# Seven PSUM banks as one tensor, and two row maxima in one VectorE instruction

## The chip, the cores and the metric

The kernel runs on one core of a Trainium2 chip. A core has a matmul engine (PE, with its weight loads shown as PEld), a vector engine (DVE), a scalar engine (ACT), a general engine (POOL) and a queue engine for transfers (SP). Each works through its own instructions in order, and they meet through counters (semaphores): an instruction can wait until another engine's count has reached a value. Matmuls write into PSUM, which has eight banks of 512 f32 columns for each of 128 partitions. DVE and ACT read from there.

The metric is the device time of one execution in microseconds. The times of before are 2018.37, 2018.74 and 2018.93 us, median 2018.74.

## What is computed

One transformer block with adaptive layer norm. Six vectors come from `silu(c) @ w_mod`. Attention follows a modulated layer norm; then a mixing MLP with shifted channels follows another one.

```python
# S = 2048 tokens, D = 512, 32 heads of 16
h = layernorm(x) * (1 + ca) + sa
q, k, v = split_heads(h @ wqkv)                 # 32 x 2048 x 16 each
p = softmax(q @ k.T / 4)                        # 32 x 2048 x 2048
x = x + ga * (merge_heads(p @ v) @ wo)
h = layernorm(x) * (1 + cb) + sb
x = x + gb * mixer_and_mlp(h)                   # w1, shift, w2, w3, w4
```

The inputs make scores large, so the softmax subtracts the maximum of each row.

## The kernel before

There are three stages. A prologue norms and transposes x, makes the modulation and projects the first heads. The attention stage takes nearly three quarters of the time. The last stage, the tail, runs the output projection and the MLP.

Attention works on 64 units: four chunks of 512 queries times 16 pairs of heads. A unit has 16 steps `s`, one for each 128 keys, and in each step the two heads `j = 0, 1`. So there are 2048 half steps. For each of them two matmuls are made, on different halves of PE's rows:

- the maximum part (`max_part`, line 980): 128 queries times 512 keys into a bank called `mb` (line 996), from which DVE takes the maximum over the keys into one column of `mx` (line 992). It runs 24 steps (`LEAD`) ahead, since a unit's 32 maxima columns must be joined (`max_fin`, line 1029) and put into the query tile before its scores are made.
- the score part (`score_part`, line 998): 128 keys times 512 queries into a bank called `sc` (line 1012), of which ACT makes the exponential as int32 into a slot of `pt` (line 1008).

The int32 has a high half that is used as it is and a low half that must be turned to f16 first (`p_low`, line 1048): POOL does so for most steps (line 1061) and ACT for the others. Value matmuls then gather both halves in a bank `pv` of their own (lines 1083 and 1086); at the end of a unit ACT copies it out, four small matmuls `ot` add the parts, and ACT, DVE and POOL write the heads' output.

The program writes the order itself. A block is three half steps: three rows (`row_pair`, line 1014) of one maximum matmul and one score matmul, then the value matmuls of two blocks earlier. A class `Sched` keeps a modelled time for each engine. From these it decides when a block starts, whether a low half goes to POOL or ACT (`g > a + LACT`) and where other work, the fill, comes between blocks: projections of later heads, weight preparation, and at the end the first piece of the tail. `Slots` (line 305) keeps for each of the seven banks the modelled time from which it is free; any free bank will do, and each use makes a new tile with the tag of its bank:

```python
def bank(nm):
    x = sm.take()
    return x, ap_.tile([P, CH], F32, name=nm, tag=f"s{x}", bufs=1)
```

Fill work takes its banks from the same seven while attention runs (`dbank`, line 425). The eighth bank is `pv`.

The semaphore waits are not written in the kernel. The building layer derives them from which tile each instruction reads and writes.

Of the kernel before, what the change touches and what calls it, by code (L numbers as in the profile page):

```python
# [96 lines left out]
XCOPY = 0  # L97
NQ = 7
NPT = 6
NV = 3  # L100
DBW, DLAT = 360.0, 2200.0
NST = 4
# [9 lines left out]
class Sched:  # L112
# [29 lines left out]
    def chain(self, *ops, prio=1, ready=None, bank=None):  # L142

        if ready is None:
            ready = self.T["P"] + PX
        n = 0
        while n < len(self.chains) and self.chains[n][2] <= prio:
            n += 1
        bank = bank is not None and id(bank.tensor)
# [100 lines left out]
    def share(self, slots, most):  # L250

        self.avail, self.back, self.owner = [], [], {}
        self.slots, self.most = slots, most

    def take(self, tile):

        if self.slots:
            i = self.slots.take()
            self.slots.t[i] = LATE
        else:  # L260
            i = self.avail.pop(0)
        b = tile(i)
        self.owner[id(b.tensor)] = i
        self.open = id(b.tensor)
        return b

    def free(self, b):

        i = self.owner.pop(id(b.tensor), None)
# [35 lines left out]
class Slots:  # L305
# [7 lines left out]

    def late(self):
        return sum(t == LATE for t in self.t)


def cA(n=CH):
# [12 lines left out]
def kernel(ctx, tc, A_x, A_wqkv, A_wo, B_w1, B_w2, B_w3, B_w4, c, w_mod, out):  # L331
# [641 lines left out]
    sm = Slots(NSM)  # L973
    e_exp, e_hi, e_low, v_free, acs = {}, {}, {}, [0.0], []

    def bank(nm):
        x = sm.take()
        return x, ap_.tile([P, CH], F32, name=nm, tag=f"s{x}", bufs=1)

    def max_part(m, j):  # L980

        u, i = divmod(m, 16)
        c, g = divmod(i, 4)
        if u not in mxs:
            mxs[u] = at.tile([P, 2, 4, NC], F32, name="mx", tag="mx", bufs=2)
        x, b = bank("mb")
        ready, sm.t[x] = sm.t[x], LATE
# [3 lines left out]
        def after(e):  # L991
            end = sch.crit("D", 605, e + PX, lambda: dve.reduce_max(mxs[u][:, j, g, c:c + 1], b, axis=AX.X))  # L992
            sm.t[x] = end + XP["D"]
            if (c, g, j) == (NC - 1, 3, 0):
                max_fin(u)
        return ready, lambda: te.matmul(b, lhs, kst[u % 3][r, c * CH:(c + 1) * CH], start=True, stop=True), after  # L996

    def score_part(s, j):

        u, kt = divmod(s, NKT)  # L1000
        if j == 0:
            pt[s] = at.tile([P, 2, CH], I32, name="pt", tag="pt", bufs=NPT)
        x, b = bank("sc")
        ready, sm.t[x] = sm.t[x], LATE
        r = slice(64 * j, 64 * j + 64)

        def after(e):
            ea = sch.crit("A", 480, e + PX, lambda: act.activation(pt[s][:, j], b, AF.Exp))  # L1008
            sm.t[x] = ea + XP["A"]
            if j:  # L1010
                e_exp[s] = e_hi[s] = ea
        return ready, lambda: te.matmul(b, kst[u % 3][r, kt * P:(kt + 1) * P], qst[u][r], start=True, stop=True), after  # L1012

    def row_pair(s, j):

        parts = []
        if 0 <= s < NS:
            parts.append((j, score_part(s, j)))
        if s + LEAD < NS:
            parts.append((1 - j, max_part(s + LEAD, 1 - j)))  # L1020
        parts = [x for _, x in sorted(parts, key=lambda x: x[0])]

        def mms():
            for _, mm, _ in parts:
                mm()
        e = sch.put("P", CROW, max(x[0] for x in parts), mms)
        return [partial(x[2], e) for x in parts]

    def max_fin(u):
        mf = at.tile([P, 8], F32, name="mf", tag="mf", bufs=2)  # L1030
        nm = at.tile([P, 2, 8], F32R, name="nm", tag="nm", bufs=2)
        mx = mxs.pop(u)

        def shift_rows():
            for j in range(2):
                for i in range(2):
                    r = 64 * j + 62 + i
                    for h in range(2):
                        sch.dma(dma.dma_start,
                                qst[u][r:r + 1, h * 256:(h + 1) * 256].bitcast(F32).rearrange("o (p l) -> o p l", l=2),  # L1040
                                nm[:, i, 4 * j + 2 * h:4 * j + 2 * h + 2].bitcast(F32))
        sch.chain(("D", 85, lambda: dve.reduce_max(mf.rearrange("p (j g) -> p j g", j=2), mx, axis=AX.X)),
                  ("A", 100, lambda: act.activation(mf, mf, AF.Copy, scale=-1.0, bias=PEXP)),
                  ("A", 100, lambda: act.activation(nm[:, 0], mf, AF.Copy)),
                  ("G", 250, lambda: pool.tensor_tensor(nm[:, 1], mf, nm[:, 0], op=OP.subtract)),
                  (None, 0, shift_rows), mark(("shift", u)), prio=0, ready=sch.T["D"])

    def p_low(s):

        p = pt[s].rearrange("p j n -> p (j n)")  # L1050
# [17 lines left out]
    def pv_part(s, lo):  # L1068
# [7 lines left out]
        def mms():  # L1076
            for j in range(2):
                for i in range(2):
                    r = 64 * j + 32 * i
                    if lo:  # L1080
                        c = 128 + 32 * j + (0 if i else 8)
                        n = min(32, 192 - c)
                        te.matmul(acc[r:r + n, :], v[:, kt + i, c:c + n].bitcast(F16), pt[s + i].bitcast(F16)[:, j, 0::2],  # L1083
                                  start=False, stop=kt == NKT - 2, skip_group_check=True)
                    else:
                        te.matmul(acc[r:r + 32, :], v[:, kt, r:r + 32], pt[s].bitcast(F16)[:, j, 1::2],  # L1086
                                  start=kt == 0, stop=False, skip_group_check=True)
        e = sch.put("P", CCOL, 0.0, mms)
        if lo:
            for i in range(2):  # L1090
                pt.pop(s + i)
                e_low.pop(s + i)
            if kt == NKT - 2:
                acs.append((u, e + COUT))
# [507 lines left out]
    for k, blk in enumerate(blocks + [[]] * (LAG + CPER)):  # L1602
# [21 lines left out]
        banks = sorted(sm.t)  # L1624
        n = 0
        for s, i in row:
            n += (s >= 0) + (s + LEAD < NS)

            start = max(start, banks[n - 1 + 2 * (s < 0)] - t)
            t += CROW  # L1630
        t += CMID
        for s, i in col:
            start = max(start, pv_ready(s, i) - t)
# [2 lines left out]
        sch.flush(need)  # L1636
        sch.T["P"] = max(sch.T["P"], start) + CIN
        low = sorted(e_exp)
        for s, i in row:
            for fn in row_pair(s, i):  # L1640
                fn()
        for x in blk[1:]:
            if x % 2 == 0:
                before(x // 2)
# [86 lines left out]
```

## Time and profile before

| what | value |
|---|---|
| median of three runs | 2018.74 us |
| profiled execution, span | 2019.7 us |
| attention, first maximum to last small sum | 96.6 to 1536.5 us |
| PE busy | 1934.4 us, 96% |
| DVE busy | 1656.3 us, 82% |
| ACT busy | 1510.2 us, 75% |
| POOL busy | 1571.9 us, 78% |
| single maxima on DVE | 2048, 1250.0 us |
| exponentials on ACT | 2048, 1060.9 us |
| low halves on POOL and on ACT | 953, 1248.3 us, and 71 |

Busy times count an engine's records without overlap. The ends of matmuls are modelled, so 96% is not PE at its peak. A group's mean is the length of one record; busy time over count is what one costs in a stream where records overlap. Idle time stands with what ended it.

### The profile page before, as it was taken

How to read it: one execution, taken by the hardware profiler on the slowest of the kernel's cores; microseconds unless marked ns; L12 is line 12 of the kernel's file. 1: busy time of each engine (PE TensorE's matmuls, PEld its weight loads, DVE VectorE, ACT ScalarE, POOL GpSimd, SP SyncE). 2: the span in 40 equal slices, each digit the busy share in tenths (PEclk: the TensorE clock that was granted, in tenths of full speed). 3: DMA queues.
4: the chain of work that ended last, by engine and by line, in shares of the span. 5: the costliest groups of instructions: out<-in, count | busy, mean ns of one | idle time of the engine just before them, and what ended most of it. 6: DMA issues, size and time to landing. Idle time of an engine off the chain costs nothing.

```text
span 2019.7 us, 41655 instructions
## 1 busy us (share of the span) xinstructions
PE 1934.4 (96%) x14456; PEld 1162.1 (58%) x14456; DVE 1656.3 (82%) x2979; ACT 1510.2 (75%) x3085; POOL 1571.9 (78%) x1488
## 2 busy tenths in 40 slices
PE   7999999999999999999999999999998999999999
PEld 5755545454444444444444444444455878898998
DVE  6398888879999999999999999999975886556443
ACT  6438987768999999999999999999985544344443
POOL 6349988879999999999999999999996554435222
PEclk9989999999999999999999999999999999999999
DMA  8777675445343434444443435354414676553541
GB/s 295 233 204 192 151 187 155 135 130 124 86 92 87 91 88 83 96 82 97 81 98 75 104 72 107 72 136 126 99 46 158 230 261 265 226 200 116 201 153 68
DMA packets 185508, 278.01 MB, mean 138 GB/s; under 512 B 117104, under 2 KB 127856, under 8 KB 169008
## 3 DMA queue, kind: packets, MB, share of 16 engines
q1 hardware_dynamic: 181792, 267.20, 49.1%
q10 hardware_dynamic: 2304, 4.20, 0.6%
q0 software_dynamic: 1200, 3.93, 0.5%
q8 instruction: 115, 1.88, 0.4%
q14 instruction: 97, 0.79, 0.1%
HBM read 211.81 MB, written 62.91 MB: 136 GB/s over the span
## 4 chain that ended last, share of the span: by engine, by line
PE 61%; DVE 16%; ACT 9%; issue 6%; POOL 4%; DMA 3%; SPq 0%; ACTq 0%; POOLq 0%; DVEq 0%
PE mb L996 13%; DVE mx L992 12%; PE pv L1086 9%; PE sc L1012 8%; ACT pt L1008 7%; PE w L363 5%; PE w L359 5%; PE w L361 5%; PE pv L1083 4%; PE ot L1113 3%; POOL pt L1061 2%; PE xT L1247 1%; POOL trs L1356 1%; PE v L359 1%; DMA wr<-Ws 1%
## 5 line engine op out<-in xcount | busy, mean ns | idle before, releaser
L1061 POOL TENSOR_SCALAR pt<-pt 128x1024 f16<-128x1024 uint16 x953 | 1248.3, 1367 | 79.9 <-ACT pt L1008 76.7
L992 DVE TENSOR_REDUCE mx<-mb 128x1 f32<-128x512 f32 x2048 | 1250.0, 681 | 72.7 <-PE mb L996 63.5
L1008 ACT ACTIVATE pt<-sc 128x512 int32<-128x512 f32 x2048 | 1060.9, 614 | 123.5 <-PE mb L996 97.1
L996 PE MATMUL mb<-kst,qtl 62*128 62x512 f32 x2048 | 781.1, 461 | 20.5 <-ACT pt L1008 10.0
L1012 PE MATMUL sc<-qtl,kst 64*128 64x512 f32 x2048 | 739.3, 449 | 4.6 <-DVE mx L992 1.8
L996 PEld LDWEIGHTS mb<-kst,qtl 62*128 62x128 f32 x2048 | 358.9, 193 | 233.7 <-ACT pt L1008 160.4
L1012 PEld LDWEIGHTS sc<-qtl,kst 64*128 64x128 f32 x2048 | 336.6, 185 | 185.4 <-DVE mx L992 118.7
L1086 PE MATMUL pv<-pt,vst 128*32 128x512 f16 x4096 | 384.8, 397 | 20.6 <-ACT ac L1103 20.6
L1460 POOL TENSOR_TENSOR g<-sq,g 128x256 fp32r<-128x256 f32 (+1 forms) x124 | 96.8, 785 | 188.9 <-ACT g L1459 176.6
L1083 PE MATMUL pv<-pt,vst 128*32 128x512 f16 (+1 forms) x2048 | 220.8, 389 | 2.5 <-POOL pt L1061 2.4
L1086 PEld LDWEIGHTS <-vst 128*32 128x32 bf16 x4096 | 91.8, 93 | 227.2 <-issue 208.8
L361 PE MATMUL w<-A,wr 128*128 128x256 f32 (+1 forms) x520 | 153.4, 295 | 0.3 <-DVE A L349 0.3
L359 PE MATMUL w<-A,wr 128*128 128x256 f32 (+1 forms) x520 | 153.2, 295 | 0.3 <-ACT A L353 0.3
L363 PE MATMUL w<-A,wr 128*128 128x256 f32 (+1 forms) x520 | 153.1, 294 | 0.0
L1456 ACT ACTIVATE sq<-w 128x256 f32<-128x256 f32 (+1 forms) x130 | 52.1, 401 | 127.0 <-PE w L363 117.5
L363 PE MATMUL w<-wr,g 128*128 128x512 f32 x270 | 106.5, 394 | 3.1 <-POOL g L1460 3.1
L359 PE MATMUL w<-wr,g 128*128 128x512 f32 x270 | 106.9, 396 | 1.8 <-DMA wr<-Ws 1.8
L361 PE MATMUL w<-wr,g 128*128 128x512 f32 x270 | 106.1, 393 | 0.0
L1438 DVE SCALAR_TENSOR_TENSOR sq<-sq,w 128x256 f32<-128x256 f32 (+1 forms) x130 | 58.1, 449 | 56.5 <-ACT sq L1458 56.3
L359 PEld LDWEIGHTS w<-A,wr 128*128 128x128 f32 x520 | 98.7, 190 | 1.7 <-ACT A L353 0.5
L361 PEld LDWEIGHTS w<-A,wr 128*128 128x128 f32 x520 | 98.7, 190 | 1.6 <-DVE A L349 0.5
L363 PEld LDWEIGHTS w<-A,wr 128*128 128x128 f32 x520 | 98.6, 190 | 0.5 <-issue 0.5
(156 smaller groups left out, 2131.6 us busy)
## 6 DMA issues: line engine op xcount, KB each, us to landing
wr<-Ws SPq DMA_DIRECT2D x66, 1024.0 KB, 5.2
vst<-Vs SPq DMA_DIRECT2D x64, 768.0 KB, 5.7
kst<-Ks SPq DMA_DIRECT2D x126, 384.0 KB, 6.1
Ws<-wr SPq DMA_DIRECT2D x14, 1024.0 KB, 5.0
qtl<-Qs SPq DMA_DIRECT2D x128, 96.0 KB, 4.3
Vs<-vt SPq DMA_DIRECT2D x32, 384.0 KB, 4.2
Ks<-qk SPq DMA_DIRECT2D x16, 512.0 KB, 3.8
Qs<-qk SPq DMA_DIRECT2D x16, 512.0 KB, 3.0
```

Source lines behind the costliest of these rows:

```text
L359: te.matmul(o, lh, rh, start=first, stop=False)
L361: te.matmul(o, lh, rl, start=False, stop=False)
L363: te.matmul(o, ll, rh, start=False, stop=last)
L992: end = sch.crit("D", 605, e + PX, lambda: dve.reduce_max(mxs[u][:, j, g, c:c + 1], b, axis=AX.X))
L996: return ready, lambda: te.matmul(b, lhs, kst[u % 3][r, c * CH:(c + 1) * CH], start=True, stop=True), after
L1008: ea = sch.crit("A", 480, e + PX, lambda: act.activation(pt[s][:, j], b, AF.Exp))
L1012: return ready, lambda: te.matmul(b, kst[u % 3][r, kt * P:(kt + 1) * P], qst[u][r], start=True, stop=True), after
L1061: e_low[s] = XP["G"] + sch.crit("G", 1345, ready, lambda: pool.tensor_scalar(o, i, 0.5, 1.0, op0=OP.mult, op1=OP.mult))
L1083: te.matmul(acc[r:r + n, :], v[:, kt + i, c:c + n].bitcast(F16), pt[s + i].bitcast(F16)[:, j, 0::2], start=False, stop=kt == NKT - 2, skip ...
L1086: te.matmul(acc[r:r + 32, :], v[:, kt, r:r + 32], pt[s].bitcast(F16)[:, j, 1::2], start=kt == 0, stop=False, skip_group_check=True)
L1113: te.matmul(b[:, t * n:(t + 1) * n], ac[:, t * P:(t + 1) * P], smat.rearrange("p j d -> p (j d)"), start=True, stop=True)
L1460: ("G", cG(n), lambda: pool.tensor_tensor(lo, sq, hi, op=OP.subtract)), (None, 0, end), bank=b)
```

## The change

The seven banks become one PSUM tensor `psb` of seven slices of 512 columns. Maxima, scores and fill work all use slices of it. The six `pt` buffers become slots of one tensor `pts` in the same way.

In a block's three half steps the maxima are grouped: one goes alone, and two are put into adjacent slices and read by one reduction over `[128, 2, 512]` into two columns of `mx`. Its columns are put in a new order, so that the two lie side by side. `place` looks for slices that let the block start earliest, and `choose` falls back to three single maxima if pairing would start the block more than 150 ns later by the model (`DTOL`). Exponentials stay single (`DSC = 0`). The readers are put down after their last matmul; a pair of maxima comes after the second of its rows.

```diff
+DMX, DSC = 1, 0
+DTOL = 150.0
...
+    def key(self, b):
+        return id(b.tensor), b.offset
...
-        return sch.take(lambda i: psd["d"].tile([P, CH], F32, name=n, tag=f"s{i}" if psd["s"] else f"d{i}", bufs=1))
+        return sch.take(lambda i: psb[:, i] if psd["s"] else psd["d"].tile([P, CH], F32, name=n, tag=f"d{i}", bufs=1))
...
-    pv, pt = {}, {}
+    pv = {}
+    psb = ap_.tile([P, NSM, CH], F32, name="psb")
+    pts = at.tile([P, NPT, 2, CH], I32, name="pts")
...
+    def max_out(x, ts, e):
+
+        n = len(ts)
+        u, i = divmod(ts[0][0], 16)
+        o = 2 * i + 1 - ts[0][1]
+        b = psb[:, x:x + n]
+        end = sch.crit("D", 72 + 533 * n, e + PX, lambda: dve.reduce_max(mxs[u][:, o:o + n], b, axis=AX.X))
+        sm.t[x:x + n] = [end + XP["D"]] * n
+        if o + n == 32:
+            max_fin(u)
+
+    def score_out(x, ts, e):
+
+        n = len(ts)
+        s, j = ts[0]
+        o = 2 * (s % NPT) + j
+        p = pts.rearrange("p a j n -> p (a j) n")[:, o:o + n]
+        ea = sch.crit("A", 53 + 427 * n, e + PX, lambda: act.activation(p, psb[:, x:x + n], AF.Exp))
+        sm.t[x:x + n] = [ea + XP["A"]] * n
...
+    def groups_of(row, two):
+
+        ms = [(k, (s + LEAD, 1 - j)) for k, (s, j) in enumerate(row) if s + LEAD < NS]
+        ss = [(k, x) for k, x in enumerate(row) if x[0] >= 0]
+        out = []
+        for tiles, fn, fin, on, cut in ((ms, max_tile, max_out, DMX, lambda x: x[0] % NKT == 0 and x[1]),
+                                        (ss, score_tile, score_out, DSC, lambda x: x[0] % NPT == 0 and not x[1])):
+            i = 0
+            while i < len(tiles):
+                n = 2 if two and on and (len(tiles) - i) % 2 == 0 and not cut(tiles[i + 1][1]) else 1
+                out.append((tiles[i:i + n], fn, fin))
+                i += n
+        return sorted(out, key=lambda x: -len(x[0]))
+
+    def choose(row):
+
+        best = None
+        for two in (1, 0):
+            gs = groups_of(row, two)
+            st, xs = sm.place([[CIN + CROW * k for k, _ in ts] for ts, _, _ in gs], sch.T["P"])
+            if best is None or st + DTOL < best[0]:
+                best = st, gs, xs
+        return best
...
+        sch.chain(("D", 85, lambda: dve.reduce_max(mf.rearrange("p (j g) -> p j g", j=2),
+                                                   mx.rearrange("p (c g j) -> p j g c", g=4, j=2), axis=AX.X)),
...
+        if row:
+            row_pairs(row, *choose(row)[1:])
```

Counted in the built program, 2048 single maxima become 724 single ones and 662 pairs. The low halves that go to ACT fall from 71 to 17, and those on POOL rise from 953 to 1007. Matmuls and exponentials keep their number. `psb` is used by 8566 instructions; in the order in which they are put down its use passes from one engine to another 5625 times (2116 turns of PE, 2087 of ACT, 1423 of DVE).

Three places follow, as the program is built, with the counters that each instruction waits for. `PE_49`, `DVE_49`, `Activation_49` and `Pool_49` count the instructions of these engines, a `DMAHW` counter those of a transfer queue.

DVE in attention, before:

```order
L992 TENSOR_REDUCE mx<-mb 128x1 [waits DVE_49,PE_49]
L992 TENSOR_REDUCE mx<-mb 128x1 [waits PE_49]
L1042 TENSOR_REDUCE mf<-mx 128x8 [waits DVE_49,Pool_49]
L992 TENSOR_REDUCE mx<-mb 128x1 [waits PE_49] x30
L1128 RECIPROCAL rc<-sm 128x8 [waits Activation_49,Pool_49]
```

DVE in attention, now (`mx<-psb 128x2` is a pair):

```order
L1032 TENSOR_REDUCE mx<-psb 128x1 [waits PE_49,Activation_49]
L1032 TENSOR_REDUCE mx<-psb 128x2 [waits Activation_49]
L1032 TENSOR_REDUCE mx<-psb 128x1 [waits PE_49]
L1032 TENSOR_REDUCE mx<-psb 128x2 [waits PE_49,Activation_49]
L1108 TENSOR_REDUCE mf<-mx 128x8 [waits DVE_49]
L1032 TENSOR_REDUCE mx<-psb 128x1 [waits Activation_49]
L1032 TENSOR_REDUCE mx<-psb 128x2 [waits Activation_49]
```

Single maxima and pairs alternate, and a maximum now waits for ACT in many places where it waited for PE.

ACT in attention, before:

```order
L1008 ACTIVATE pt<-sc 128x512 [waits PE_49,Pool_49]
L1008 ACTIVATE pt<-sc 128x512 [waits PE_49] x3
L1008 ACTIVATE pt<-sc 128x512 [waits PE_49,Pool_49]
L1008 ACTIVATE pt<-sc 128x512 [waits PE_49]
L1008 ACTIVATE pt<-sc 128x512 [waits PE_49,Pool_49]
```

ACT in attention, now:

```order
L1043 ACTIVATE pts<-psb 128x512 [waits PE_49,Pool_49]
L158 ACTIVATE pts<-pts 128x1024 [waits Activation_49]
L1043 ACTIVATE pts<-psb 128x512 [waits DVE_49]
L1043 ACTIVATE pts<-psb 128x512 [waits PE_49,Pool_49]
L1043 ACTIVATE pts<-psb 128x512 [waits DVE_49]
L1043 ACTIVATE pts<-psb 128x512 [waits PE_49,Pool_49]
L1043 ACTIVATE pts<-psb 128x512 [waits DVE_49,PE_49]
```

An exponential now waits for DVE in many places where it waited for PE. (The `Pool_49` waits are for the slot that the exponential writes.)

PE, the three rows of a block, before and now (`kst` and `qtl` are the key and query tiles):

```order
L996 MATMUL mb<-kst_147,qtl_145 128x512 [waits Activation_49]
L1012 MATMUL sc<-qtl_1103,kst_1105 128x512 [waits DVE_49] x2
L996 MATMUL mb<-kst_147,qtl_145 128x512 [waits Activation_49] x2
L1012 MATMUL sc<-qtl_1103,kst_1105 128x512 [waits DVE_49]
L1086 LDWEIGHTS vst
```

```order
L1018 MATMUL psb<-kst_1063,qtl_1061 128x512 [waits DVE_49]
L1024 MATMUL psb<-qtl_965,kst_967 128x512
L1024 MATMUL psb<-qtl_965,kst_967 128x512 [waits Activation_49]
L1018 MATMUL psb<-kst_1063,qtl_1061 128x512
L1018 MATMUL psb<-kst_1063,qtl_1061 128x512 [waits Activation_49]
L1024 MATMUL psb<-qtl_965,kst_967 128x512
L1153 LDWEIGHTS vst
```

Before, each matmul waited for its own bank's reader; now the first matmul of each row waits and the second has no wait of its own.

More of the change, by code (lines that the diff above doesn't have):

```diff
@@ L148, in chain @@
             n += 1
-        bank = bank is not None and id(bank.tensor)
+        bank = bank is not None and self.key(bank)
         if bank == self.open:
@@ L315, in late, with place, go @@
         return sum(t == LATE for t in self.t)
+    def place(self, groups, now):
+        n = len(self.t)
+        best = [None, None]
+        def go(k, used, out, start, late):
+            if best[0] and start > best[0][0]:
+                return
+            if k == len(groups):
+                if best[0] is None or (start, late) < best[0]:
+                    best[:] = [(start, late), out]
+                return
+            offs = groups[k]
+            for i in range(n - len(offs) + 1):
+                if any(i + x in used for x in range(len(offs))):
+                    continue
+                st, lt = start, late
+                for x, o in enumerate(offs):
+                    st = max(st, self.t[i + x] - o)
+                    lt += self.t[i + x]
+                go(k + 1, used | {i + x for x in range(len(offs))}, out + [i], st, lt)
+        go(0, frozenset(), [], now, 0.0)
+        return (best[0][0] if best[0] else 2 * LATE), best[1]
 def cA(n=CH):
@@ L1090, in pv_part @@
             for i in range(2):
-                pt.pop(s + i)
                 e_low.pop(s + i)
@@ L1623 @@
         sch.flush(need)
[L1624 to L1630, printed above, removed]
+        if row:
+            start = choose(row)[0]
+            if s0 < 0:
+                start = max(start, sorted(sm.t)[need + 1] - t - CROW * (len(row) - 1))
+        t += CROW * len(row)
         t += CMID
```

80 lines of the change are left out of this document (35 added, 45 removed).

## The prediction

> **What bounds the kernel now.** I read the busy time by stretch first, to find the stage that the change touches. The columns are the stretch, its length, the busy time and instructions of PE, weight loads, DVE, ACT and POOL, the granted TensorE clock, and the DMA share and rate.
>
> ```profile
> 500.00:1450.00 950.00, 921.00 (x7837) 436.12 (x7830) 912.05 (x1587) 879.18 (x1743) 911.95 (x777) 1.00 0.44 94
> 96.60:1536.50 1439.90, 1393.33 (x11340) 690.01 (x11341) 1315.07 (x2281) 1245.82 (x2496) 1325.19 (x1137) 0.99 0.48 111
> 1536.50:2019.70 483.20, 457.58 (x2698) 409.36 (x2697) 294.16 (x589) 210.19 (x484) 201.00 (x286) 0.99 0.53 192
> ```
>
> Attention (first maximum to last small sum) is 1439.9 of the span's 2019.7 us, and in its steady part DVE, POOL, ACT and PE are all busy 93 to 97%: they run side by side. The groups of that part show what each does.
>
> ```profile
> L992 DVE TENSOR_REDUCE mx<-mb 128x1 f32<-128x512 f32 x1493 | 907.7, 681 | 31.6 <-PE mb L996 25.3 <-PE sc L1012 3.1
> L1061 POOL TENSOR_SCALAR pt<-pt 128x1024 f16<-128x1024 uint16 x684 | 890.4, 1363 | 32.8 <-ACT pt L1008 30.2
> L1008 ACT ACTIVATE pt<-sc 128x512 int32<-128x512 f32 x1493 | 770.0, 615 | 54.5 <-PE mb L996 44.9 <-PE sc L1012 2.2 <-POOL pt L1061 0.8
> L996 PE MATMUL mb<-kst,qtl 62*128 62x512 f32 x1493 | 574.8, 460 | 10.6 <-ACT pt L1008 6.9
> ```
>
> 1493 maxima are 497.7 blocks of three, so a block takes 950 / 497.7 = 1.91 us. A maximum costs DVE 907.7 / 1493 = 0.608 us of throughput, although a single one is recorded as 0.681: neighbours overlap at their ends. In the same way an exponential is 0.615 alone and 0.516 in the stream, and a POOL product 1.302. DVE fills 1.82 of the 1.91 us, POOL 1.85. The waits of the same stretch say how close the coupling is.
>
> ```profile
> PEld mb L996 <- ACT pt L1008: 137.4, 404, 0.8
> PEld sc L1012 <- DVE mx L992: 99.6, 258, 0.5
> ```
>
> PE waits for banks, 0.3 to 0.4 us at a time, so PE has slack. The kernel is bound by DVE and POOL, and it lives on ACT, DVE and PE working on different banks at the same time.
>
> **The change, part by part.**
>
> *The pair.* 662 pairs replace 1324 single maxima. A second 512 columns cannot cost more than a second instruction (0.608) or, in my reading of 0.681 alone against 0.608 streamed, much less than 0.53 (0.608 less the 0.073 by which two records overlap). So a pair saves DVE 0 to 0.075 us, at most 662 x 0.075 = 50 us of busy time.
>
> *POOL.* The order moves 54 of the 71 low-half products that ACT had taken back to POOL: 54 x 1.302 = 70 us more POOL work. If everything else stayed as it is, POOL would need 1.5 x 47/48 x 1.302 = 1.91 us a block plus what else it does (911.95 - 890.4 = 21.6 us in 497.7 blocks, 0.04), 1.95 in all against 1.91.
>
> *The one tensor.* This decides. In the rows of the order shown with the change, an exponential waits for DVE and a maximum for ACT; before, each of them waited for PE alone (and for the buffer it writes). I resolved every such wait to the instruction whose count it names. In all 5625 places where the use of `psb` passes from one engine to another, the first instruction of the new engine waits for the last one of the old, and about nine in ten of these waits join accesses to different banks. Readers wait for readers. So the seven banks are used by one engine at a time: row of matmuls, exponential, row, pair, exponential, row, and so on. What ran side by side is now a sum: 2116 turns of PE, and on ACT and DVE 2048 exponentials, 724 single maxima, 662 pairs and some 190 evictions of other work. That sum is what I price.
>
> *A turn of PE.* Here is a row of two matmuls at full clock, whose readers were waiting, and an exponential that released PE (time order: start, duration, engine, line, what).
>
> ```profile
> 534.16 0.18 PEld L1012 LDWEIGHTS sc<-qtl,kst 64*128 64x128 f32 x1 [0.45 <-DVE mx L992]
> 534.16 0.50 PE L1012 MATMUL sc<-qtl,kst 64*128 64x512 f32 x1
> ...
> 534.73 0.69 DVE L992 TENSOR_REDUCE mx<-mb 128x1 f32<-128x512 f32 x1 [0.42 <-PE mb L996]
> ...
> 534.76 0.60 ACT L1008 ACTIVATE pt<-sc 128x512 int32<-128x512 f32 x1 [0.42 <-PE mb L996]
> ```
>
> ```profile
> 1002.41 0.60 ACT L1008 ACTIVATE pt<-sc 128x512 int32<-128x512 f32 x1
> ...
> 1003.06 0.19 PEld L996 LDWEIGHTS mb<-kst,qtl 62*128 62x128 f32 x1 [0.30 <-ACT pt L1008]
> ```
>
> From PE's start to the waiting reader: 0.57 us to DVE, 0.60 to ACT, call it 0.585. An exponential alone takes 0.60 and PE starts 0.05 after its end: 0.65 a turn. I give DVE the same 0.05: 0.73 for a single maximum; and 0.681 + 0.53 + 0.05 = 1.26 for a pair (between 1.15, if it paid nothing but columns, and 1.41, twice a lone one).
>
> But the clock matters, because PE will mostly idle. Four neighbouring stretches of the clock's own length, and the row of matmuls in the slow one:
>
> ```profile
> 723.35:726.76 3.41, 3.41 (x34) 1.54 (x34) 3.41 (x7) 3.00 (x7) 3.41 (x4) 1.00 1.02 193
> 726.76:730.17 3.41, 2.25 (x22) 1.42 (x22) 2.23 (x4) 3.02 (x5) 2.50 (x3) 1.00 0.97 216
> 730.17:733.58 3.41, 3.41 (x17) 1.78 (x16) 2.52 (x5) 2.26 (x5) 2.99 (x4) 0.50 0.18 72
> 733.58:736.99 3.41, 3.41 (x34) 1.50 (x32) 3.38 (x8) 2.97 (x9) 2.74 (x3) 1.00 0.00 0
> ```
>
> ```profile
> 730.19 0.28 PEld L1012 LDWEIGHTS sc<-qtl,kst 64*128 64x128 f32 x1
> 730.19 0.79 PE L1012 MATMUL sc<-qtl,kst 64*128 64x512 f32 x1
> ...
> 731.05 1.89 DVE L992 TENSOR_REDUCE mx<-mb 128x1 f32<-128x512 f32 x3 [0.17 <-PE mb L996]
> 731.08 1.58 ACT L1008 ACTIVATE pt<-sc 128x512 int32<-128x512 f32 x3 [0.49 <-PE mb L996]
> ...
> 732.32 0.29 PEld L996 LDWEIGHTS mb<-kst,qtl 62*128 62x128 f32 x1 [0.44 <-ACT pt L1008]
> ...
> 733.15 1.29 DVE L992 TENSOR_REDUCE mx<-mb 128x1 f32<-128x512 f32 x2 [0.21 <-PE sc L1012]
> ```
>
> A stretch with 22 matmuls in place of 34 was followed by one at half clock; there a row takes 0.83 to 0.86 us to DVE and 0.89 to ACT, 0.865 as I use it. Half clock ended after a stretch of 17 slow but unbroken matmuls. In the changed kernel a block holds 6 row matmuls, 9 of the values and 0.4 small ones. With 6.6 us a block (below) that is 8 in 3.41 us, far under the 22 that lost the clock and the 17 that regained it. I take half clock through nearly all of attention.
>
> The Trainium skill ("TensorE: Matmul & The Clock Gate", section "Part 1: The HAM clock gate (the "warmup" mystery)") says that the gate falls to half rate after a whole idle window of about 3.4 us. Read so, PE, which works every two microseconds, would keep its full clock; the trace differs, since the stretch before 730.17 was busy for 2.25 of 3.41 us. What that reading would make of the time is the second rival.
>
> *Other work in the chain.* Projection and weight work of the first quarter takes its banks from `psb` too and stands in the chain: 312 matmuls of 512 columns, 252 of 256, 256 small ones. Two rows of the stream, and the small eviction:
>
> ```profile
> 97.83 0.28 PE L361 MATMUL v<-wp,hT 128*128 128x256 f32 x1
> ...
> 97.95 0.28 PE L363 MATMUL v<-wp,hT 128*128 128x256 f32 x1
> ```
>
> ```profile
> L1120 ACT ACTIVATE sm<-ot 128x136 f32<-128x136 f32 x47 | 13.4, 285 | 14.5 <-PE ot L1113 14.4
> ```
>
> 0.12 us for 256 columns, so 0.24 for 512, and double at half clock: 312 x 0.48 + 252 x 0.24 + 256 x 0.11 = 238 us. About 190 evictions at 0.29 to 0.6: 80 us.
>
> *The sum for attention:* PE turns 2116 x 0.865 = 1830; other matmuls 238; exponentials 2048 x 0.65 = 1331; single maxima 724 x 0.73 = 529; pairs 662 x 1.26 = 834; evictions 80. Together 4842 us. Over 699 blocks (683 of three scores each, and 16 at the start with maxima alone) that is 6.9 us with the extra work, 6.6 without (3 rows 2.6, 3 exponentials 1.95, a single and a pair 1.99). I take off 20 us for about 110 evictions that follow another on the same engine and overlap it by some 0.1 to 0.2. The value matmuls do not touch `psb`: per block nine, in groups of four side by side, about 1.1 us even at half clock (two and a quarter groups at twice the 0.23 between the two below). They lie behind the block's last row, under its exponential and maximum (0.65 + 1.26 = 1.9, or 0.65 + 0.73 = 1.4), so they cost nothing; without that cover they would be 1.1 us a block. POOL's 1.95 us a block and the loads lie under 6.6 as well.
>
> ```profile
> 1000.20 0.40 PE L1083 MATMUL pv<-pt,vst 128*32 128x512 f16 x4
> ...
> 1000.43 0.41 PE L1086 MATMUL pv<-pt,vst 128*32 128x512 f16 x4
> ```
>
> What lies outside attention, 2019.7 - 1439.9 = 579.8 us, stays. So 579.8 + 4822 = 5402 us against the profiled 2019.7; the median of the runs shown is 1 us less than that execution, so **about 5400 us**, 2.7 times the time before.
>
> **The rivals.**
>
> *The clock holds or returns.* Same chain, PE turns at 0.585: 1238, other matmuls 133, sum 4125, time 4705. For it: a stretch with 20 matmuls that kept the clock in the next one.
>
> ```profile
> 1153.37:1156.78 3.41, 2.32 (x20) 1.11 (x17) 3.41 (x6) 3.23 (x6) 3.15 (x3) 1.00 1.07 178
> 1156.78:1160.19 3.41, 3.34 (x32) 2.11 (x31) 2.57 (x5) 3.03 (x7) 2.75 (x3) 1.00 0.77 235
> ```
>
> So the edge lies near 20 to 22; against the rival stands that 8 is far below it. A clock that falls and returns lies between, around 5050; denser stretches of the first quarter may do that.
>
> *Banks stay independent after all, and it is not slower.* If a wait named only the bank's last user, the sum would not exist. DVE would need 1.82 - 0.075 x 0.97 = 1.75 us a block, and were the block to follow DVE, 683 x 0.07 = 50 us would come off at most: 1970 to 2019. It decides at the first exponential that starts while a maximum on another bank still runs. For it is only that the data allow it. Against it are the waits themselves, on both engines, with the counts of neighbours on other banks.
> The Trainium skill ("PSUM — Partial Sum Buffer", section "PSUM bank collisions raise a hardware error ⚠️") says that engines need to be kept apart per bank and quadrant, readers included. By it this rival would be what the chip needs; no run here shows the rule, and the program in hand waits by tensor.
>
> *Banks independent, POOL the bound.* As the last, with 1.95 us a block on POOL: 683 x 0.04 = 27 us more at the least, 2045, or 2080 if POOL stays 97% busy as now.
>
> *More than the chain.* A value matmul that waits for POOL late, or a read of `pv` by ACT, could stand in front of a row. 64 units with 1 us each would be 64 us; this is inside the upper end.
>
> **How the numbers follow.** Chain at half clock 0.66; chain at full or changing clock 0.29; banks independent with POOL the bound 0.02; not slower 0.03. The likeliest case by itself: pairs from 1.15 to 1.41 give -73 to +99 us, PE turns from 0.83 to 0.89 (the ends seen above) -74 to +53, other matmuls at full clock -105, exponentials up to 0.02 longer +40; not all at once, so 5220 to 5570. The range reaches down through the full-clock case to 4680 and up to 5570. About 0.2% is what a measurement of this kernel can tell from no change; faster 0.02, within 0.01, slower 0.97.
>
> **What would show it.** Right: blocks about 6.6 us apart in the steady part; maxima and exponentials that never overlap in time; waits of ACT for DVE and of DVE for ACT among the longest, which the waits before do not have; PE's turn 0.86 us and a granted clock near 0.5; POOL busy under a third. If the clock is 1.00 and blocks are 5.8 us apart, the mechanism is right and the PE term too large. Wrong: exponentials and maxima side by side and blocks near 1.9 us, with DVE or POOL over 90% busy.

## The result, and the profile after

The changed kernel takes 5532.72 us (median of four runs, 5532.08 to 5534.19), against 2018.84 us for the kernel before in the same session. It is slower by a factor of 2.739, 95% interval 2.734 to 2.744. The prediction was 5400 us, with a range of 4680 to 5570; the case that it held likeliest had 5220 to 5570 by itself.

The profiled execution has a span of 5530.3 us, and attention goes from 95.5 to 5041.5 us: 4946 us, where the sum had 4822. The remaining 584 us are what they were (580). The stretches of the kernel after, with the same columns as before (length, then busy time and instructions of PE, weight loads, DVE, ACT and POOL, then granted clock, DMA share and rate):

```profile
1000.00:2000.00 1000.00, 549.22 (x2290) 198.38 (x2282) 279.86 (x318) 271.05 (x482) 284.74 (x235) 0.50 0.12 29
2000.00:3000.00 1000.00, 538.02 (x2314) 185.77 (x2312) 287.03 (x327) 282.99 (x501) 295.46 (x244) 0.50 0.11 25
95.50:5041.50 4946.00, 2723.86 (x11336) 1016.58 (x11336) 1392.43 (x1619) 1362.10 (x2442) 1429.35 (x1194) 0.51 0.13 32
```

Of engines that were 93 to 97% busy, DVE, ACT and POOL are now busy 27 to 30% of the time in these two stretches. The clock is 0.50. The groups of the second of these stretches show the pace:

```profile
L1018 PE MATMUL psb<-kst,qtl 62*128 62x512 f32 x441 | 348.8, 791 | 235.2 <-DVE mx L1032 178.1 <-ACT pts L1043 55.0 <-DMA qtl<-Qs 2.1
L1032 DVE TENSOR_REDUCE mx<-psb 128x1 f32<-128x512 f32 (+1 forms) x299 | 282.6, 945 | 704.4 <-ACT pts L1043 385.0 <-PE psb L1024 319.4
L1043 ACT ACTIVATE pts<-psb 128x512 int32<-128x512 f32 x441 | 263.2, 597 | 653.2 <-DVE mx L1032 339.9 <-PE psb L1018 201.0 <-PE psb L1024 112.4
```

441 rows are 147 blocks, 6.80 us each, against 1.91 before. The work of DVE and ACT has not become longer: an exponential takes 0.597 us where it took 0.615. PE's has, at half the clock: 0.791 us for a maximum's matmul where it was 0.460. What grew most is the idle time. The longest waits of the whole kernel (engine, line, what it waited for; total, times, longest):

```profile
POOL pts L1128 <- ACT pts L1043: 2758.5, 873, 40.6
DVE mx L1032 <- ACT pts L1043: 1749.1, 659, 5.9
PEld psb L1024 <- ACT pts L1043: 1589.5, 1002, 3.8
ACT pts L1043 <- DVE mx L1032: 1569.8, 629, 5.4
```

POOL waits for exponentials, as it did before, only far longer. New is that DVE waits for ACT and ACT for DVE, although neither reads what the other writes here: the maxima and the exponentials read different banks. A piece of the time order shows it (start, duration, engine, line, what, and the idle time before):

```profile
2504.18 0.60 ACT L1043 ACTIVATE pts<-psb 128x512 int32<-128x512 f32 x1 [0.46 <-PE psb L1018]
2504.80 0.69 DVE L1032 TENSOR_REDUCE mx<-psb 128x1 f32<-128x512 f32 x1 [2.21 <-ACT pts L1043]
...
2505.55 0.79 PE L1018 MATMUL psb<-kst,qtl 62*128 62x512 f32 x1 [1.48 <-DVE mx L1032]
...
2505.55 0.79 PE L1024 MATMUL psb<-qtl,kst 64*128 64x512 f32 x1
2506.39 0.60 ACT L1043 ACTIVATE pts<-psb 128x512 int32<-128x512 f32 x1 [1.62 <-PE psb L1024]
2507.04 0.28 PEld L1024 LDWEIGHTS psb<-qtl,kst 64*128 64x128 f32 x1 [1.20 <-ACT pts L1043]
```

Exponential, maximum, row, exponential, row: one engine at a time, with 0.02 to 0.06 us between the end of one and the start of the next. In the whole trace no maximum and no exponential overlap in time; in the kernel before it happens 4057 times.

### The profile page after: what moved, and what is told of

Read it like the earlier page. It is cut to its first block, busy times and chain, and to the rows that moved or that the text cites. A ratio compares the mean times of both kernels' runs of the same rounds, so it can differ in the third digit from the quotient of the medians.

```text
span 5530.3 us, 42016 instructions
## 1 busy us (share of the span) xinstructions
PE 3271.0 (59%) x14456; PEld 1494.5 (27%) x14456; DVE 1733.2 (31%) x2317; ACT 1627.3 (29%) x3031; POOL 1676.0 (30%) x1542
## 4 chain that ended last, share of the span: by engine, by line
PE 39%; DVE 23%; ACT 22%; issue 4%; DMA 1%; POOL 0%; ACTq 0%; DVEq 0%; SPq 0%; POOLq 0%
DVE mx L1032 22%; ACT pts L1043 21%; PE psb L1024 14%; PE psb L1018 14%; PE psb L1179 2%; PE w L392 2%; PE w L388 2%; PE w L390 2%; PE psb L388 1%; PE psb L392 1%; PE psb L390 1%; ACTq L1043 0%; DMA wr<-Ws 0%; PE xT L1313 0%; ACT sm L1186 0%
## 5 line engine op out<-in xcount | busy, mean ns | idle before, releaser
L1032 DVE TENSOR_REDUCE mx<-psb 128x1 f32<-128x512 f32 (+1 forms) x1386 | 1311.8, 946 | 3258.7 <-ACT pts L1043 1749.1
L1018 PE MATMUL psb<-kst,qtl 62*128 62x512 f32 x2048 | 1599.9, 786 | 1076.8 <-DVE mx L1032 791.6
L1128 POOL TENSOR_SCALAR pts<-pts 128x1024 f16<-128x1024 uint16 x1007 | 1345.4, 1338 | 2866.1 <-ACT pts L1043 2758.5
L1024 PE MATMUL psb<-qtl,kst 64*128 64x512 f32 x2048 | 1607.1, 785 | 978.4 <-ACT pts L1043 964.4
L1043 ACT ACTIVATE pts<-psb 128x512 int32<-128x512 f32 x2048 | 1222.5, 597 | 3099.8 <-DVE mx L1032 1569.8
L1018 PEld LDWEIGHTS psb<-kst,qtl 62*128 62x128 f32 x2048 | 576.1, 283 | 1632.9 <-DVE mx L1032 1133.7
L1024 PEld LDWEIGHTS psb<-qtl,kst 64*128 64x128 f32 x2048 | 578.1, 282 | 1622.3 <-ACT pts L1043 1589.5
L1153 PE MATMUL pv<-pts,vst 128*32 128x512 f16 x4096 | 598.3, 613 | 0.0
L1150 PE MATMUL pv<-pts,vst 128*32 128x512 f16 (+1 forms) x2048 | 327.9, 627 | 1.1 <-POOL pts L1128 1.1
L390 PEld LDWEIGHTS w<-A,wr 128*128 128x128 f32 x504 | 96.9, 192 | 1.5 <-DVE A L378 0.4
```

The lines of the kernel that those rows point to most:

```text
L390: te.matmul(o, lh, rl, start=False, stop=False)
L1032: end = sch.crit("D", 72 + 533 * n, e + PX, lambda: dve.reduce_max(mxs[u][:, o:o + n], b, axis=AX.X))
L1043: ea = sch.crit("A", 53 + 427 * n, e + PX, lambda: act.activation(p, psb[:, x:x + n], AF.Exp))
L1128: e_low[s] = XP["G"] + sch.crit("G", 1345, ready, lambda: pool.tensor_scalar(o, i, 0.5, 1.0, op0=OP.mult, op1=OP.mult))
L1153: te.matmul(acc[r:r + 32, :], v[:, kt, r:r + 32], pt(s).bitcast(F16)[:, j, 1::2], start=kt == 0, stop=False, skip_group_check=True)
```

## The experiments

Ten kernels were run, each beside the kernel before on the same chip. In what follows, "the changed kernel" is the one of the diff above, and the time of the kernel before is that of the same session.

**One tensor alone.** The kernel before, with nothing changed but that its seven banks are slices of one tensor:

```diff
+    psb = ap_.tile([P, NSM, CH], F32, name="psb")
...
-        return x, ap_.tile([P, CH], F32, name=nm, tag=f"s{x}", bufs=1)
+        return x, psb[:, x]
```

> The kernel before with one edit: its seven banks become slices of one tensor. Order, single maxima, tiles of the exponentials and choice of banks stay as before; there are no pairs and no new planner. One-tensor theory: the same chain as in the changed kernel, with 2085 turns of VectorE in place of 1423 because every maximum is alone: PE 2180 us, ACT 1365, DVE 2048 x 0.735 + 40 = 1545, and 584 outside, so 5670 us (5550 to 5800), slower than the change itself. Rival, that the pairs (1.2 us long, in neighbouring banks) or the planner cost the time: 2020 us.

Measured: 5634.3 us (one run) against 2019.2, within what was expected. No pair, no new order, no shared `pts`, and it takes 2.79 times as long.

```profile
ACT pt L1012 <- DVE mx L996: 2172.2, 946, 5.8
DVE mx L996 <- ACT pt L1012: 2169.4, 986, 5.5
```

```profile
2000.00:3000.00 1000.00, 526.35 (x2266) 181.16 (x2266) 302.64 (x459) 292.90 (x503) 270.96 (x225) 0.50 0.12 25
```

The same two waits and the same half clock. The one tensor is enough to make all of the loss. The changed kernel is 102 us faster than this one: it has 662 fewer DVE turns (1423 against 2085), which by the prediction's prices (2 x 0.73 - 1.26 = 0.20 us) is worth 132. By the trace all DVE turns add up to 1416 us in the changed kernel and to 1539 here, 123 more. Inside the chain the pair does pay.

**Everything but the one tensor, without pairs.** The changed kernel with seven tensors of one bank, and single maxima; its planner, the column order of `mx` and the one tensor `pts` stay:

```diff
-DMX, DSC = 1, 0
+DMX, DSC = 0, 0
...
-    psb = ap_.tile([P, NSM, CH], F32, name="psb")
+    psbs = [ap_.tile([P, 1, CH], F32, name=f"psb{i}", tag=f"s{i}", bufs=1) for i in range(NSM)]
```

> The changed kernel with seven tensors of one bank each and, since a pair needs two banks of one tensor, single maxima; its planner, its order of columns and its one tensor of exponential slots stay. One-tensor theory: no wait names another bank's user any more, so the speed of before: 2000 to 2050 us. Rival, that the planner or the one tensor of exponential slots costs a good part: above 3000 us.

Measured: 2041.7 us, ratio 1.0117 (1.0097 to 1.0136). In the steady part DVE, ACT and POOL are busy 91 to 94% again:

```profile
500.00:1450.00 950.00, 906.31 (x7664) 427.72 (x7662) 896.52 (x1552) 866.34 (x1703) 893.25 (x760) 0.99 0.44 92
```

So the slots of `pts`, though one tensor too, let ACT, POOL and PE work on different slots at once: what serialises is `psb`. What is left of the change (planner, column order, one `pts`) costs 22 us (1462 maxima in this stretch, where there were 1493). Which part of it does so was not tried.

**Pairs in tensors of their own.** The changed kernel with five places: two tensors of two banks for pairs, three of one. A place is taken whole, so a score or a single maximum can hold two banks. The planner was fitted to this: a pair may also be the first two of a block's three maxima, and a block asks for five places at most.

```diff
+UNITS = (2, 2, 1, 1, 1)
...
-    psb = ap_.tile([P, NSM, CH], F32, name="psb")
+    psbs = [ap_.tile([P, n, CH], F32, name=f"psb{i}", tag=f"s{i}", bufs=1) for i, n in enumerate(UNITS)]
```

> The changed kernel with five tensors in place of one: two of two banks, three of one bank. A pair of maxima takes one of the first two; a score or single maximum takes any, and a tensor is used by one of them at a time, so that no wait names another bank's user. 682 pairs stay. One-tensor theory: a pair by itself is harmless, and the time is near that of before; it has five places in place of seven, so rows wait a little more: 1990 to 2120 us. Rival, that the pair itself makes the time: above 3000 us.

Measured: 2092.4 us, ratio 1.0357 (1.0339 to 1.0374). The pairs are there, 682 of them (662 in the changed kernel), the chain is gone, and the kernel is still slower than before. In the steady part, with forms kept apart for DVE:

```profile
L1030 DVE TENSOR_REDUCE mx<-psb 128x2 f32<-128x1024 f32 x480 | 584.5, 1218 | 18.6 <-PE psb L1022 7.7 <-PE psb L1016 4.7 <-ACT pts L1041 0.5
L1030 DVE TENSOR_REDUCE mx<-psb 128x1 f32<-128x512 f32 x479 | 327.1, 683 | 23.4 <-PE psb L1016 6.5 <-PE psb L1022 0.8
```

```profile
L1030 DVE TENSOR_REDUCE mx<-psb 128x2 f32<-128x1024 f32 (+1 forms) x959 | 862.2, 951 | 42.1 <-PE psb L1016 11.3 <-PE psb L1022 8.6 <-ACT pts L1041 0.5
L1128 POOL TENSOR_SCALAR pts<-pts 128x1024 f16<-128x1024 uint16 x706 | 913.7, 1366 | 10.0 <-ACT pts L1041 9.9
```

480 pairs and 479 singles are 479.7 blocks. DVE needs 862.2 / 479.7 = 1.797 us for each, where three singles need 3 x 0.608 = 1.824: against the single maxima of the kernel before the pair saves 0.027 us a block, not the 0.075 that was its upper bound. POOL, with 706 products and 10 us of idle time, looked like the bound, as in the prediction's third rival. The next two runs took work off POOL to see.

**Was it POOL?** The last kernel, with one low half in ten given to ACT (99 in place of 20); and as its control the kernel before with the same rule (106 in place of 71):

```diff
-        if g > a + LACT:
+        if g > a + LACT or s % 10 == 5 and 40 < s < 1010:
```

> Edit: the run with pairs in two-bank tensors of their own, with one low-half product in ten given to ACT whatever the planner says (99 in all in place of 20). Theory: the 2092 us there were POOL's. POOL had 1.47 products a block x 1.294 us = 1.905 us, with its other work 1.94 of a block of 1.98. With one in ten on ACT it needs 1.35 x 1.294 + 0.04 = 1.78 us; DVE with 862.2 us in 479.7 blocks (1.80 us) is then the fullest engine, and the block falls back to about 1.90 us: 2030 to 2055 us in all. Rival: the block is held by where the pairs can be put (five places in place of seven), and POOL is only full beside it: no change, 2085 to 2100 us. Second rival: the pair is worth its 0.075 us a block after all once POOL is out of the way: below 2015 us.

> Edit: the kernel before, with the same rule of one low-half product in ten on ACT (106 in all in place of 71). It is the control for the run above. Theory: before, DVE (1.82 of 1.91 us) and POOL (1.85) are about equally full, so taking 0.07 us a block from POOL alone buys little: 2005 to 2025 us. Rival: POOL alone bounds the kernel before: 683 blocks x 0.05 us = 35 us less, 1985 us.

Measured: 2138.7 us, ratio 1.0579 (1.0555 to 1.0604), and 2048.5 us, ratio 1.0135 (1.0111 to 1.0158). Both expectations fell, and on the side that none had named: with less to do on POOL both kernels became slower, by 46 us (45 by the two ratios) and 27 us. The groups and a wait of the first of the two:

```profile
L1128 POOL TENSOR_SCALAR pts<-pts 128x1024 f16<-128x1024 uint16 x628 | 820.8, 1357 | 87.5 <-ACT pts L1041 84.6 <-ACT mf L1110 1.0 <-POOL osb L1190 0.2
L159 ACT ACTIVATE pts<-pts 128x1024 f16<-128x1024 uint16 x70 | 95.8, 1369 | 0.0
```

```profile
POOL pts L1128 <- ACT pts L1041: 84.6, 141, 1.3
```

POOL has become idle (87.5 us in place of 10.0) while it waits for ACT's exponentials. A low half on ACT takes 1.37 us, the time of more than two exponentials in the queue behind it. That these are what POOL then waits for fits the rows, but was not tested apart from this. So what is shown is only that giving one product in ten to ACT does not pay. Whether POOL held the kernel with pairs back stays open, since the work that left POOL went into the very queue that POOL waits for. The trace of that kernel speaks on both sides. POOL is busy 931.6 us there, 98%, or 1.94 us a block, and with this work on POOL no block can be shorter than that; 1.98 was measured. But little is seen to wait for POOL's products in the same stretch:

```profile
DVE rc L1194 <- POOL pts L1128: 4.1, 6, 1.0
ACT pts L1041 <- POOL pts L1128: 2.1, 3, 0.9
```

**Was it the pair instruction?** The kernel with five places, each pair read by two single maxima one after the other, with the same places for the banks:

```diff
...
-        lambda: dve.reduce_max(mxs[u][:, o:o + n], b, axis=AX.X)
+        lambda: [dve.reduce_max(mxs[u][:, o + k:o + k + 1], b[:, k], axis=AX.X) for k in range(n)][-1]
```

> Edit: the run with pairs in two-bank tensors of their own (2092 us), with each pair read by two single maxima, one after the other, in place of one instruction; places, order and all else stay. Theory: DVE spends 1.797 us a block there against 3 x 0.608 = 1.824 with single maxima, so the pair instruction is worth 0.027 us a block at most, and what makes that kernel slower than before is how its banks are bound together in twos: 2085 to 2115 us. Rival: the pair instruction itself holds the kernel back (a bank pair comes free only after 1.22 us, where a single one is free after 0.68): 2030 to 2060 us, like the run with singles in banks of their own (2042).

Measured: 2119.2 us, ratio 1.0473 (1.0446 to 1.0501): 27 us slower than with the pair instruction (23 by the two ratios), and a little over the upper end given. So the instruction is worth about 25 us here, 0.04 us a block. DVE's own row in the steady part:

```profile
L1030 DVE TENSOR_REDUCE mx<-psb 128x1 f32<-128x512 f32 x1415 | 880.6, 683 | 26.4 <-PE psb L1022 8.1 <-PE psb L1016 5.3 <-PE pv L1153 0.3
```

1415 single maxima are 471.7 blocks, 1.867 us each. Against this control the pair spares DVE 0.07 us a block, of which the kernel's time shows about half. What makes these kernels slow is the binding of banks in twos, with the places, the order and the planner's rules that go with it: without the pair instruction they are 72 to 78 us above the run with single banks (2041.7). These parts were not tried one by one.

**Neighbours in twos.** The kernel before, bank numbers handed out as before, with tensors of two, two, two and one banks:

```diff
+    psbs = [ap_.tile([P, min(2, NSM - i), CH], F32, name=f"psb{i}", tag=f"s{i}", bufs=1) for i in range(0, NSM, 2)]
...
-        return x, ap_.tile([P, CH], F32, name=nm, tag=f"s{x}", bufs=1)
+        return x, psbs[x // 2][:, x % 2]
```

> Edit: the kernel before, with its seven banks as four tensors of two, two, two and one banks; bank numbers are handed out as before, no pairs. Only neighbours in one tensor now wait for each other. Theory (a tensor is used by one engine at a time, whatever the bank): four tensors must carry six uses a block, each some 0.5 us of matmul and 0.65 us of reader and 0.1 us between, 6 x 1.25 / 4 = 1.9 us a block if they were always full, and uneven waits add half as much again: 2.4 to 2.9 us a block, 2350 to 2700 us, with the granted clock near 1. Rival: what costs is any sharing of a tensor by two engines, so it is as slow as the seven in one: above 5000 us. Second rival: sharing by twos is free: 2020 us.

Measured: 3491.7 us, ratio 1.727 (1.722 to 1.733). This lies between the two rivals, as the theory says of a cost that grows with the number of banks in a tensor, but far above its 2350 to 2700. Its steady part:

```profile
1000.00:2000.00 1000.00, 823.13 (x3814) 313.85 (x3812) 486.49 (x772) 469.02 (x848) 455.06 (x378) 0.52 0.19 41
```

```profile
L1012 ACT ACTIVATE pt<-psb 128x512 int32<-128x512 f32 x726 | 409.2, 596 | 470.4 <-PE psb L1016 216.7 <-PE psb L1000 211.7 <-DVE mx L996 33.6
```

726 exponentials are 242 blocks of 4.13 us, where 2.4 to 2.9 was expected "with the granted clock near 1". The clock is 0.52, although PE is busy 82% of the time by the profile (the ends of matmuls are modelled). This is what the expectation left out. With the 0.79 us of a matmul at half clock, as in the changed kernel, in place of its 0.5, the same working gives 6 x 1.54 / 4 = 2.3 us a block, and 3.5 with half as much again. This is an estimate, and it covers most of the miss, not all; a run that holds the clock up in this kernel was not made.

**Useless matmuls to hold the clock.** The changed kernel with groups of four matmuls of zero weights into the open `pv`: three groups behind the first row of a block, two behind the second, two at the end (17,292 more matmuls, which add nothing to `pv`):

```diff
+WARM = (3, 2, 2)
...
+                    te.matmul(pv[u][r:r + 32, :], zw, mhalf.bitcast(BF16)[:, 1:2].to_broadcast([P, CH]), start=False, stop=False, skip_group_check=True)
```

> The changed kernel with more work: after each row of a block PE also runs 3, 2 and 2 groups of four side-by-side matmuls of zero weights, which add zero to the open value bank while ACT and DVE have their turns. Nothing else changes. If the half clock is what a thin PE gets, as the prediction has it, the clock comes back to 1.0 for most of attention, a turn of PE falls from 0.89 to about 0.6 us and the long turns with small matmuls are about halved: 4750 to 4950 us, faster with 20000 more matmuls. Rival, that 0.89 us is what a lone row costs whatever the clock, or that the clock does not follow the density of matmuls: 5530 us or more.

Measured: 5034.1 us (one run): 499 us less than the changed kernel, with more than twice as many matmuls. The clock in the same stretch:

```profile
2000.00:3000.00 1000.00, 734.30 (x6686) 245.49 (x6682) 317.34 (x361) 311.86 (x554) 326.57 (x270) 0.84 0.13 28
```

That is above the 4750 to 4950 expected: the clock came back only in part. The time of all PE turns, added up from the trace, fell from 2169 to 1634 us; at full clock throughout the prediction has 1371. So it lies where the prediction put "a clock that falls and returns", around 5050.

**More of them.** Five, four and four groups:

```diff
-WARM = (3, 2, 2)
+WARM = (5, 4, 4)
```

> Edit: the run with useless zero matmuls again, with groups of four after the three rows of a block five, four and four in place of three, two and two. With the fewer groups the granted clock was 0.86 and PE's turns 1634 us in all. Theory: the clock follows how much PE does in a stretch; about 11 rows and groups a block in place of 8 hold it at 0.97 or more, PE's turns go down to 1240 to 1400 us, and the time comes to 4650 to 4850 us, where the prediction put the chain at full clock (4705). Rival: each added group stands in the way of the next row as much as it gains in clock: 5000 to 5100 us at a clock above 0.9.

Measured: 5076.5 us (median of two). The rival was right.

```profile
2000.00:3000.00 1000.00, 836.96 (x10118) 323.62 (x10118) 316.25 (x359) 309.90 (x549) 324.50 (x267) 0.94 0.13 29
```

```profile
2504.60 1.05 PE L1104 MATMUL pv<-mhalf,zw 128*32 128x512 bf16 x16
2504.71 0.60 ACT L1047 ACTIVATE pts<-psb 128x512 int32<-128x512 f32 x1 [1.33 <-PE psb L1028]
...
2505.58 0.18 PEld L1028 LDWEIGHTS psb<-qtl,kst 64*128 64x128 f32 x1 [0.43 <-ACT pts L1047]
```

The clock is 0.94 and PE's turns are down to 1523 us, but the exponential here ends at 2505.31 and the row that follows it starts 0.27 us later, behind the useless matmuls, where it was 0.05. ACT's turns, to the start of the next row, add up to 1533 us in place of 1400: 133 more, where PE's are 111 less. The full-clock time of 4705 was not reached this way.

**The small matmuls.** The changed kernel with one of the four small matmuls `ot` of a unit; three quarters of that sum are left out.

```diff
+            if t == 0:
                 te.matmul(b[:, t * n:(t + 1) * n], ac[:, t * P:(t + 1) * P], ...
```

> Edit: the changed kernel, with one of the four small matmuls that join a unit's value sums; the other three quarters of that sum are left out (the copy reads old numbers there), and the rest is as it was. Theory: these matmuls stand in the chain, and 65 turns with four of them last 2.69 us in place of about 1.3: without three of four, 64 x 0.9 to 64 x 1.6 us go, 5425 to 5475 us against 5532. Rival: those turns are long for another reason (the copy that they wait for): 5520 to 5535 us.

Measured: 5452.8 us (median of two), 80 us less than the changed kernel. In the changed kernel such a turn reads:

```profile
2006.22 1.92 PE L1179 MATMUL psb<-smat,ac 128*128 128x34 f32 x8 [1.46 <-DVE mx L1032]
...
2008.07 0.79 PE L1018 MATMUL psb<-kst,qtl 62*128 62x512 f32 x1
...
2008.90 0.69 DVE L1032 TENSOR_REDUCE mx<-psb 128x1 f32<-128x512 f32 x1 [2.74 <-PE psb L1024]
```

Most such turns last 2.69 us from their start to the reader (2.68 here): four small matmuls (eight records) take 1.85 us, 0.46 each, ahead of the row's 0.84. With one matmul most of these turns last 1.41. 64 x (2.69 - 1.41) = 82 us, and 80 were measured: the small matmuls stand in the chain at this price.

## Why the prediction was right

**The one tensor decides: right.** The trace has 5626 turns (PE 2116, ACT 2087, DVE 1423), that is the 5625 hand-overs that were counted, and the run with this edit alone loses all the time. The signs that were named came: maxima and exponentials that never overlap, waits between ACT and DVE among the longest, clock 0.50, POOL busy under a third (30%).

**The sum, term by term.** DVE's and ACT's turns: 834 + 529 + 1331 + 80 - 20 = 2754 predicted, and the turns add up to 1416 + 1364 = 2780. A pair's turn was mostly 1.26 to 1.28 us (1.26 predicted), a single's 0.72 to 0.79 (0.73), an exponential's 0.63 to 0.65 (0.65). PE's turns: 1830 + 238 = 2068 predicted, 2169 measured. These 101 us, with the 26 of the others, make 127, and attention was missed by 124 (the last turns lie behind it). The step that was mis-sized is "other matmuls 238": in it "256 x 0.11" gives 28 us to all the small ones, a price for which no row was shown, while four of them take 1.85 us in front of a row, 64 x 1.85 = 118 us. The kernel before had a row for it:

```profile
L1113 PE MATMUL ot<-smat,ac 128*128 128x34 f32 x512 | 69.1, 280 | 0.0
```

With two records for each matmul that is 69.1 / 256 = 0.27 us at its clock of 0.99, and 0.46 was measured at 0.50. Rows of one maximum and one score with no other work were 0.888 us on average (0.84 or 0.91 to DVE and 0.90 to ACT are the commonest), not 0.865: 1900 x 0.023 = 44 us. By difference, the rest of the other work came out some 30 us cheaper than priced. In the steady part, where the sums of a unit fall in every 10.7 blocks, the same two terms make the step from the predicted 6.6 (its three parts add up to 6.54) to 6.80: 3 x 0.023 and 1.85 / 10.7, 0.24 us together.

**The clock: right.** In all the traces the granted clock changes at steps of 3.41 us, the length of the prediction's stretches. Three such stretches, one behind the other, in the changed kernel:

```profile
2499.00:2502.41 3.41, 2.48 (x12) 0.63 (x12) 1.04 (x1) 0.60 (x1) 1.33 (x1) 0.50 0.00 0
2502.41:2505.82 3.41, 1.06 (x4) 0.56 (x4) 0.88 (x2) 1.68 (x3) 1.33 (x1) 0.50 0.58 218
2505.82:2509.23 3.41, 2.71 (x16) 0.60 (x16) 0.67 (x1) 1.19 (x2) 1.35 (x1) 0.50 0.03 13
```

4 to 16 matmuls a stretch, below the 20 to 22 at which the kernel before began to lose the clock, and none of them is filled. In the run with the fewer useless matmuls the clock is lost near such a count again, in two stretches that follow each other (they lie 0.4 us beside the clock's steps, hence 0.94 and 0.56). Behind them stands the kind of wait with PE's longest single one in the steady part (1000 to 4500 us):

```profile
2020.46:2023.87 3.41, 1.90 (x20) 0.61 (x16) 0.87 (x2) 1.19 (x2) 1.33 (x1) 0.94 0.02 5
2023.87:2027.28 3.41, 3.17 (x24) 0.72 (x22) 0.87 (x1) 1.19 (x2) 1.34 (x1) 0.56 0.00 0
```

```profile
PE psb L1028 <- ACT pts L1047: 377.0, 505, 2.7
```

PE never waited for a whole 3.41 us there, and the clock fell again and again: a stretch with 20 matmuls, 1.90 us busy, was followed by half clock. These matmuls differ in size, so where the edge lies is not settled by their count. The Trainium skill ("TensorE: Matmul & The Clock Gate", section "Part 1: The HAM clock gate (the "warmup" mystery)") has the half rate follow a whole idle window; the measurement decides against that reading. The price of the clock is shown as well: useless matmuls alone take 499 us off.

**The cover: right, as far as the sum tells.** The sum came within 3% without a term for value matmuls, POOL's products or loads; uncovered, the value matmuls alone had been put at 1.1 us a block. With 54 more low halves, POOL is idle more than two thirds of the time.

**What the rivals said.** "The clock holds or returns", which the working on the clock calls the second rival though it stands first, did not happen. "Banks stay independent after all, and it is not slower" did not happen either; and the run with pairs in tensors of their own shows one way to have independent pairs, with five places, in which the pair is no gain. The step "a pair saves DVE 0 to 0.075 us" holds: 0.027 against the maxima of the kernel before, 0.07 against those of the control, and 0.04 by the times of the two runs with and without the instruction. "Banks independent, POOL the bound" gave 2045 to 2080 us, and 2092 came, at 1.98 us a block; whether its cause is the one is left open, since relieving POOL loaded ACT. Why the kernel with two-bank tensors and no pair instruction takes 72 to 78 us more than the one with single banks is settled no further than that it is not the instruction. A run with fewer places for single maxima, which would tell the number of places from the time that a pair's second bank waits, was not made. No run was faster than the kernel before.

## What to carry to other kernels

Before merging buffers into one tensor, ask at what grain waits on it are derived: if by tensor, every reader of one slice waits for the last user of any other, and the cost is the sum of all turns, countable from the program before a run. Look at the waits as built for this: the PSUM tensor `psb` was such a case, the tensor of slots `pts` was not, and why they differ is not shown here. Price that chain with turns (from an engine's start to the next engine's start) taken from the trace, at the clock that a thinned-out PE will be granted, and count the small matmuls that can stand in front of a row at their full length. And moving work off an engine that is 98% busy need not pay: the engine that takes it has a queue of its own, and what then waits behind the new work belongs in the price.

## What was not expected of the hardware

Adding 17,292 useless matmuls made a kernel 499 us faster, and adding 14,824 more made it 42 us slower (28 by the ratios to the kernel before), at a clock of 0.94 in place of 0.86. With two banks in a tensor the clock was 0.52 although PE was busy 82% of the time by the profile. And reading two banks with one reduction spares DVE only 0.03 to 0.07 us against two reductions in a stream, and 0.04 us of the kernel's time.
